# The last two heads of an attention kernel divided on chip, and seven output tiles spread between the scores

## The chip, the cores and the metric

One core of a Trainium2 chip (trn2) runs the kernel. The metric is the device time of one execution in microseconds (us), the median of several runs. TensorE multiplies matrices, VectorE, ScalarE and GpSimd work on vectors, and SyncE (SP) issues most of the DMA transfers.

## The reference

The inputs are fp32. With x of shape (2048, 512), 32 heads of 16 and a feed-forward width of 1792:

```python
q, k, v = (x @ wqkv) split into 3, by heads of 16
a = softmax(q @ k.T * 16 ** -0.5) @ v          # per head, over 2048 keys
a = concat(a) @ wo
b = (silu(x @ w1) * (x @ w3)) @ w2
g = sigmoid((x * gate_w).sum(-1))
out = g * a + (1 - g) * b
```

## The kernel before

Products with fp32 inputs are made of halves: an operand is split into a rounded part H and the rest L (type fp32r), and three matmuls (HH, HL, LH) are summed in one PSUM bank. The scores, the softmax numerators and the product with V take one or two passes.

**Order of TensorE's work.** A first stage transposes x and projects part of q and k and all of v. Then one long loop goes through a string of letters, `order`. Q is a score unit: two heads at once, 128 keys by 512 queries each, in a pair of PSUM banks `S`, followed by one exponential on ScalarE into a buffer `p` (there are 8). P multiplies two such units with V into the bank `acc`. F is a feed slot: it asks `feed` for one matmul in each of the two 64-row halves of TensorE (lanes 0 and 1). A long period is `one`: 8 Q, 21 F and 4 P, the P all at its end. A double period is `two`: 8 Q, 15 F and 4 P, the P in two groups. There are 1024 score units: 2 halves of the queries, 16 pairs of heads (`j`), 16 key blocks, 2 groups of queries.

**The feed.** `blocks()` lists what the slots are filled with, each block a sum over `length` matmuls: 136 blocks of 12 (the other q and k, and the gate and up products of the feed-forward part), 48 of 14 (`h_product`: 16 output tiles of the feed-forward product, in three parts each), and output tiles 0 to 7 of the attention's projection with wo, 12 matmuls each (tile 7 as two sums that run side by side, `o_half`). A block runs its rows 0 to 63 in one lane and then rows 64 to 127 in the other; a small VectorE write (`tick`) stands between the two. `done` then takes the bank away. There are three banks `f`; a block may take a bank only REST = 9 ticks of the loop's clock after the bank's last block ended (`pick`), and the second turn waits GAP = 6.

**Small work.** Everything else is tied to the count of scores: loads of K and Q (`load_step`), the silu's reciprocals in pieces of 64 columns (`small`), and `stages`, lists of steps of which one runs per score, the first list first. `divide(k, half)` divides the outputs of a group of 8 heads: denominators from `D_d`, one reciprocal, to `R_d`, back broadcast, a product on GpSimd, and to `N_d`. `rest_of_o` then fetches and splits groups 0 to 2 of the second half of the queries.

**Pairs.** `evac(j, half)` copies `acc` to `u` and stores 16 rows of output and one of denominators per head and query group.

**The end.** After the loop the last group of heads (k = 3, half 1) goes the way through DRAM (`reciprocals`, `fetch_o`), while TensorE does output tiles 8 to 15 with `three`: first groups 0 to 2 of all tiles (72 matmuls, into eight banks), then group 3 (24), and `mix` adds each tile to its feed-forward part and stores it.

Of the kernel before, what the change touches and what calls it, by code (L numbers as in the profile page):

```python
# [17 lines left out]
P = 128  # L18
# [15 lines left out]
def gated_mix_kernel(ctx: ExitStack, tc: tile.TileContext, x, wqkv, wo, w1, w3, w2, gate_w, out):  # L34
# [527 lines left out]
    def h_done(t, part):  # L562
        def done(ps):
            if part == 0:
                y_[t] = wk.tile([P, 512], F32, name=f"y{t % 2}")
                nc.vector.tensor_scalar(y_[t], ps, omg[:, t:t + 1], None, op0=OP.mult)
                return
            y = y_[t]
            nc.vector.scalar_tensor_tensor(y, ps, omg[:, t:t + 1], y, op0=OP.mult, op1=OP.add)  # L569
            if part == 1:  # L570
                return
            nc.sync.dma_start(B_d[P * t:P * t + P, :], y)
            if t in (11, 12, 13):
                load_bt(t - 11)
            if t in (4, 5, 6):
                later.append(lambda: load_wo((0, 1, 3)[t - 4]))
            if t == NT - 1:
                stages.append(rest_of_o())
        return done
# [20 lines left out]
    def fetch_o(k, b, o, r, e=nc.sync):  # L600
        e.dma_start(o, O_d[P * k:P * k + P, 512 * b:512 * b + 512])
        src = R_d[8 * k:8 * k + 8, 512 * b:512 * b + 512]
        nc.sync.dma_start(r, bass.AP(tensor=src.tensor, offset=src.offset, ap=[[S, 8], [0, DH], [1, 512]]))

    def divide(k, half):
# [18 lines left out]
        if (k, half) == (2, 1):  # L624
            load_wo(2)
# [14 lines left out]
    def o_half(t):  # L640
        def product(ps, r, n, second):
            k, i = divmod(n, 3)
            return nc.tensor.matmul(ps, ot[t][i == 1][r, P * k:P * k + P], wo_[k][i == 2][r, :],  # L643
                                    start=n == 0, stop=n == 3 * ND - 1)
# [6 lines left out]
    def first_half_done(t):  # L651
        def done(ps):
            nc.vector.scalar_tensor_tensor(bt[t], ps, g[:, t:t + 1], bt[t], op0=OP.mult, op1=OP.add)
# [13 lines left out]
    def load_o(k, b):  # L667

        if k not in Oh:
            Oh[k] = xp.tile([P, 2, 512], F32R, name=f"xH{k}")  # L670
            Ol[k] = xp.tile([P, 2, 512], F32R, name=f"xL{k}")
        halves_of(N_d[P * k:P * k + P, 512 * b:512 * b + 512], Oh[k][:, b - 2, :], Ol[k][:, b - 2, :], "fr")

    def rest_of_o():
        for k in range(ND - 1):
            for b in (2, 3):
                load_o(k, b)
                for _ in range(4):
                    yield

    def blocks():
# [14 lines left out]
        for t in range(NT // 2 - 1):  # L696
            yield o_product(t), o_done(t), 3 * ND
        t = NT // 2 - 1
        yield o_half(t), (first_half_done(t), o_done(t)), 3 * ND

    NBLOCK = 8 * len(chunks) + 3 * NT + NT // 2 + 1
    source = blocks()

    REST, GAP = 9, 6
# [53 lines left out]
    def evac(j, half):  # L758
        u = wk.tile([P, 512], F32, name="u")
# [7 lines left out]
        for gq in range(2):  # L767
            t = 1024 * half + 512 * gq
            for h in range(2):
                r = 32 * (2 * gq + h)  # L770
                hh = 2 * j + h
                last = half == 1 and j == NPAIR - 1
                (nc.scalar if last else nc.sync).dma_start(O_d[DH * hh:DH * hh + DH, t:t + 512], u[r:r + DH, :])
# [29 lines left out]
    LONG, SHORT = 80, 47  # L803
# [7 lines left out]
    for i, c in enumerate(order):  # L811
        clock += 1 if c != "P" else 4
        if c == "Q":
# [10 lines left out]
            if issued % 128 == (40 if issued // 128 == 5 else 12) and 1 <= issued // 128 < 8:  # L824
                stages.append(divide((issued // 128 - 1) % 4, (issued // 128 - 1) // 4))
            if small or later and hurry:
# [15 lines left out]
    assert lanes[0] is None  # L842
    for _ in reciprocals(ND - 1, 1):
        pass
    k = ND - 1
    orr = [(slot("fr", F32), slot("sg", F32)) for _ in range(2)]
    for b in (2, 3):
        fetch_o(k, b, *orr[b - 2], nc.scalar)
# [3 lines left out]


    banks = {}
    for t in range(NT // 2, NT):
        n, r = divmod(t - NT // 2, 2)
        if n < 2:
            if r == 0:
                both = psum2()
            banks[t] = both[:, r, :]  # L860
        else:
            banks[t] = bank() if t < NT - 1 else acc
        if r == 0:
            y = wk.tile([P, 2, 512], F32, name=f"p{free.pop(0)}")
        bt[t] = y[:, r, :]
        nc.sync.dma_start(bt[t], B_d[P * t:P * t + P, :])

    def project(t, k):
        o = P * t - 1024
        hi, lo = (x[k][:, 0:2, :].rearrange("p b t -> p (b t)")[:, o:o + P] for x in (Oh, Ol))  # L870
        three(banks[t], hi, lo, wo_[k][0], wo_[k][1], k == 0, k == ND - 1)

    for t in range(NT // 2, NT):
        for n in range(ND - 1):
            project(t, n)
    Oh[k], Ol[k] = (wk.tile([P, 2, 512], F32R, name=f"p{free.pop(0)}") for _ in range(2))
    for b in (2, 3):
        o, r = orr[b - 2]
        nc.vector.tensor_mul(o, o, r)
        nc.scalar.activation(Oh[k][:, b - 2, :], o, AF.Copy)  # L880
        nc.vector.tensor_sub(Ol[k][:, b - 2, :], o, Oh[k][:, b - 2, :])

    for n, t in enumerate((8, 10, 12, 13, 14, 15, 9, 11)):
        project(t, k)
        if n < NT // 2 - 1:
            mix(t, banks[t], (nc.sync, nc.scalar)[n % 2])
        else:
            mix(t, banks[t], nc.scalar, slice(0, D // 2))
            mix(t, banks[t], nc.sync, slice(D // 2, D))
# [27 lines left out]
```

## Time and profile before

| | |
|---|---|
| median of 3 runs | 1403.1 us (1402.82 to 1404.16) |
| the profiled execution | 1403.17 us, span 1401.4 us |
| busy share of the span | TensorE 100%, ScalarE 74%, VectorE 35%, GpSimd 23% |
| start of the last matmul | 1396.84 us |
| granted clock, mean | 1.000 |

The times come from runs of the whole program; the profile is one execution, whose span runs from its first to its last instruction. Matmuls overlap and their ends are modelled, so the distance between their starts says more than their busy share.

### The profile page before, as it was taken

What the parts mean: (1) busy time and instruction counts of PE and PEld (TensorE: products, weight loads), DVE (VectorE), ACT (ScalarE), POOL (GpSimd) and SP (SyncE); (2) the same over time, 40 slices, a digit from 0 to 9 for tenths busy, and PEclk for the clock granted to TensorE, in tenths of its full rate; (3) what the DMA queues carried; (4) which work ended last, traced back from release to release, by engine and by line L of the source; (5) the groups of instructions that cost most, each with busy time, mean ns of one, the idle gap of its engine ahead of it and who ended that gap; (6) DMA issues with size and microseconds to landing.
All of it is one profiled execution on the core that took longest, in us unless ns stands there. A gap on an engine that the chain in (4) does not pass through costs nothing.

```text
span 1401.4 us, 28854 instructions
## 1 busy us (share of the span) xinstructions
PE 1394.9 (100%) x11422; PEld 823.2 (59%) x11422; DVE 484.9 (35%) x1071; ACT 1032.5 (74%) x1153; POOL 320.9 (23%) x357
## 2 busy tenths in 40 slices
PE   9999999999999999999999999999999999999998
PEld 8866566566566565565565565565555555555556
DVE  5511111564545546555454654511101111101113
ACT  4457677777777777777777777787887788788771
POOL 6123433011011101110110116432242331323220
PEclk9999999999999999999999999999999999999999
DMA  7653554343224423223333246443443443445435
GB/s 207 170 122 93 139 135 113 73 113 77 47 56 84 114 55 83 63 67 96 70 77 68 80 80 165 115 97 79 106 113 79 109 102 62 111 104 133 107 95 178
DMA packets 112814, 141.44 MB, mean 101 GB/s; under 512 B 16416, under 2 KB 70944, under 8 KB 109600
## 3 DMA queue, kind: packets, MB, share of 16 engines
q1 hardware_dynamic: 111392, 137.42, 40.7%
q8 instruction: 92, 1.51, 0.5%
q10 hardware_dynamic: 1280, 2.10, 0.4%
q14 instruction: 50, 0.41, 0.1%
HBM read 90.70 MB, written 48.76 MB: 100 GB/s over the span
## 4 chain that ended last, share of the span: by engine, by line
PE 98%; DMA 1%; POOL 0%; SPq 0%; DVE 0%; issue 0%; DVEq 0%; POOLq 0%
PE acc L779 32%; PE f L432 26%; PE S L791 19%; PE f L550 11%; PE S L199 2%; PE f L636 1%; PE f L96 1%; PE f L98 1%; PE f L97 1%; DMA gw<-r_d 1%; PE f L643 0%; PE f L165 0%; PE acc L353 0%; DMA Kt<-kH_d 0%; PE S L96 0%; PE S L97 0%
## 5 line engine op out<-in xcount | busy, mean ns | idle before, releaser
L795 ACT ACTIVATE p<-S 128x1024 f32<-128x1024 f32 x1024 | 967.3, 1026 | 302.7 <-PE S L791 293.4
L779 PE MATMUL acc<-p,V 128*17 128x512 f32 x4096 | 473.5, 594 | 0.0
L791 PE MATMUL S<-Qt,Kt 50*128 50x512 f32 x2048 | 403.7, 407 | 0.7 <-DVE V L415 0.7
L791 PEld LDWEIGHTS S<-Qt,Kt 50*128 50x128 f32 x2048 | 183.4, 184 | 182.2 <-ACT p L795 80.3
L779 PEld LDWEIGHTS acc<-p,V 128*17 128x17 f32 x4096 | 102.5, 97 | 273.0 <-issue 273.0
L463 DVE RECIPROCAL sg<-sg 128x64 f32<-128x64 f32 x448 | 209.6, 517 | 51.2 <-issue 49.2
L432 PE MATMUL f<-xH,fl 64*128 64x512 f32 x1088 | 218.0, 392 | 0.1
L432 PE MATMUL f<-xL,fh 64*128 64x512 f32 x1088 | 218.0, 392 | 0.0
L432 PE MATMUL f<-xH,fh 64*128 64x512 f32 x1088 | 217.1, 390 | 0.0
L432 PEld LDWEIGHTS f<-xH,fl 64*128 64x128 f32 x1088 | 105.0, 186 | 24.3 <-POOL fl L329 0.5
L432 PEld LDWEIGHTS f<-xL,fh 64*128 64x128 f32 x1088 | 105.1, 186 | 22.3
L432 PEld LDWEIGHTS f<-xH,fh 64*128 64x128 f32 x1088 | 104.3, 185 | 23.4
L752 DVE MEMSET tick<- 1x1 f32 x191 | 11.3, 59 | 271.1 <-PE f L550 151.2
L328 POOL CAST fh<-fr 128x512 fp32r<-128x512 f32 x34 | 21.9, 645 | 356.4 <-DMA fr<-in_B_w_dram 241.4
L550 PE MATMUL f<-xH,fl 64*128 64x512 f32 x208 | 74.1, 390 | 0.0
L550 PE MATMUL f<-xL,fh 64*128 64x512 f32 x208 | 71.9, 390 | 0.0
L550 PE MATMUL f<-xH,fh 64*128 64x512 f32 x208 | 70.5, 391 | 0.0
L455 DVE COPY gs<-f 128x512 f32<-128x512 f32 x56 | 38.7, 691 | 69.8 <-PE f L432 63.5
L569 DVE SCALAR_TENSOR_TENSOR y<-f,omg,y 128x512 f32<-128x512 f32 x32 | 24.0, 752 | 107.4 <-PE f L550 107.4
L550 PE MATMUL f<-xH,raw 64*128 64x512 f32 x192 | 59.3, 390 | 0.0
L619 POOL TENSOR_TENSOR hx<-hx,gw 128x512 f32<-128x512 f32 x8 | 10.3, 1287 | 198.3 <-DMA gw<-r_d 187.9
L461 DVE TENSOR_SCALAR sg<-sg 128x512 f32<-128x512 f32 x56 | 26.2, 468 | 83.1 <-ACT sg L460 78.9
(214 smaller groups left out, 1339.7 us busy)
## 6 DMA issues: line engine op xcount, KB each, us to landing
Kt<-kH_d SPq DMA_DIRECT2D x128, 128.0 KB
h_d<-sg SPq DMA_DIRECT2D x56, 256.0 KB
sg<-h_d SPq DMA_DIRECT2D x43, 256.0 KB
fr<-in_B_w_dram SPq DMA_DIRECT2D x42, 256.0 KB
Qt<-qH_d SPq DMA_DIRECT2D x128, 64.0 KB
Kt<-kL_d SPq DMA_DIRECT2D x64, 128.0 KB
Qt<-qL_d SPq DMA_DIRECT2D x64, 64.0 KB
b_d<-y SPq DMA_DIRECT2D x16, 256.0 KB
```

The costliest lines, as they stand in the source:

```text
L96: nc.tensor.matmul(ps, sH, mH, start=first, stop=False)
L199: nc.tensor.matmul(ps[:, i, :], w[i][h][:, k, :], xs[b][:, k, :], start=n == 0, stop=n == len(order) - 1)
L328: nc.gpsimd.tensor_copy(hi, src)
L432: return nc.tensor.matmul(ps, w[i == 1][r, k, :], (xL if i == 2 else xH)[b][r, k, :], start=n == 0 and not second, stop=n == 3 * ND - 1 an ...
L455: nc.vector.tensor_copy(gs, ps)
L461: small.append(lambda: nc.vector.tensor_scalar(sg, sg, 1.0, None, op0=OP.add))
L463: small.append(lambda q=q: nc.vector.reciprocal(sg[:, q:q + 64], sg[:, q:q + 64]))
L550: ins = nc.tensor.matmul(ps, hs[t][q][i == 1][r, P * o:P * o + P], (w2L if i == 2 else w2H)[q][r, o, :], start=n == 0 and not second, stop ...
L569: nc.vector.scalar_tensor_tensor(y, ps, omg[:, t:t + 1], y, op0=OP.mult, op1=OP.add)
L779: nc.tensor.matmul(acc[r:r + DH + 1, :], V[:, k, 2 * j + h, :], p[:, h, :], start=k == 0, stop=k == NT - 1)
L791: nc.tensor.matmul(ps[:, h, :], Kt[i][r:r + 50, P * k:P * k + P], Qt[i][r:r + 50, t:t + 512], start=True, stop=True)
L795: nc.scalar.activation(p, ps, AF.Exp, scale=SCALE)
```

## The change

LONG goes from 80 to 90 and SHORT from 47 to 37. REST goes from 9 to 7. Output tile 7 becomes an ordinary block. Tiles 8 to 14 enter the feed with the first three of four groups of heads (LATE = 9 matmuls; tile 14 as two sums side by side), and their sums are added into `bt`, which `rest_of_o` loads. wo's block 2 is loaded by `later`. The last group of heads is divided in two ways: heads 24 to 29 by `six_heads` inside the loop, through DRAM; heads 30 and 31 (rows 96 to 127 of the group) after the loop, without DRAM: `acc` is copied to `u`, turned by transposes so that the queries are on partitions, divided there, turned back and split. The end does all of tile 15 and the last group of tiles 8 to 14.

```diff
-            if t in (4, 5, 6):
-                later.append(lambda: load_wo((0, 1, 3)[t - 4]))
+            if t in (4, 5, 6, 7):
+                later.append(lambda: load_wo((0, 1, 3, 2)[t - 4]))
...
-        if (k, half) == (2, 1):
-            load_wo(2)
...
-    def o_half(t):
+    def part_product(t, turns):
         def product(ps, r, n, second):
             k, i = divmod(n, 3)
-            return nc.tensor.matmul(ps, ot[t][i == 1][r, P * k:P * k + P], wo_[k][i == 2][r, :],
-                                    start=n == 0, stop=n == 3 * ND - 1)
+            return nc.tensor.matmul(ps, o_rows(t, k, i == 1)[r, :], wo_[k][i == 2][r, :],
+                                    start=n == 0 and not second, stop=n == LATE - 1 and (second or not turns))
         return product
 
...
+    sums = None
+
+    def part_done(t):
         def done(ps):
-            nc.vector.scalar_tensor_tensor(bt[t], ps, g[:, t:t + 1], bt[t], op0=OP.mult, op1=OP.add)
+            add = lambda: nc.vector.scalar_tensor_tensor(bt[t], ps, g[:, t:t + 1], bt[t], op0=OP.mult, op1=OP.add)
+            add() if sums is None else sums.append(add)
         return done
...
+    def o_rows(t, k, low):
+        x = (Ol if low else Oh)[k]
+        b, o = divmod(P * t - 1024, 512)
+        return x[:, b, o:o + P]
 
     def rest_of_o():
+        for n, x in zip("HL", (Oh, Ol)):
+            for m in range(2):
+                both = xp.tile([P, 4, 512], F32R, name=f"x{n}{m}")
+                x[2 * m], x[2 * m + 1] = both[:, 0:2, :], both[:, 2:4, :]
+        for m, n in enumerate("HL"):
+            rows = xp.tile([P, 4, 512], F32, name=f"x{n}2")
+            for i in range(4):
+                bt[NT // 2 + 4 * m + i] = rows[:, i, :]
         for k in range(ND - 1):
             for b in (2, 3):
-                load_o(k, b)
+                halves_of(N_d[P * k:P * k + P, 512 * b:512 * b + 512], Oh[k][:, b - 2, :], Ol[k][:, b - 2, :], "fr")
                 for _ in range(4):
                     yield
+        for t in range(NT // 2, NT):
+            nc.sync.dma_start(bt[t], B_d[P * t:P * t + P, :])
+            yield
+
+    def six_heads():
+
+        k, rr = ND - 1, slice(0, 6 * DH)
+        rows = lambda d: d[8 * k:8 * k + 6, 1024:2048].rearrange("h (a t) -> h a t", a=16)
+        nc.sync.dma_start(dd[rr], rows(D_d))
+        for _ in range(5):
+            yield
+        nc.vector.reciprocal(dd[rr], dd[rr])
+        yield
+        nc.sync.dma_start(rows(R_d), dd[rr])
+        both = wk.tile([P, 2, 512], F32, name="od")
+        pairs = [(both[:, 0, :], both[:, 1, :]), (slot("fr", F32), slot("sg", F32))]
+        for b in (2, 3):
+            o, r = pairs[b - 2]
+            nc.sync.dma_start(o[rr], O_d[P * k:P * k + 6 * DH, 512 * b:512 * b + 512])
+            src = R_d[8 * k:8 * k + 6, 512 * b:512 * b + 512]
+            nc.sync.dma_start(r[rr], bass.AP(tensor=src.tensor, offset=src.offset, ap=[[S, 6], [0, DH], [1, 512]]))
+        for _ in range(6):
+            yield
+        for b in (2, 3):
+            o, r = pairs[b - 2]
+            nc.gpsimd.tensor_mul(o[rr], o[rr], r[rr])
+            split(Oh[k][rr, b - 2, :], Ol[k][rr, b - 2, :], o[rr])
+            yield
 
...
-        for t in range(NT // 2 - 1):
+        for t in range(NT // 2):
             yield o_product(t), o_done(t), 3 * ND
-        t = NT // 2 - 1
-        yield o_half(t), (first_half_done(t), o_done(t)), 3 * ND
-
-    NBLOCK = 8 * len(chunks) + 3 * NT + NT // 2 + 1
+        for t in range(NT // 2, NT - 2):
+            yield part_product(t, True), part_done(t), LATE
+        yield part_product(NT - 2, False), (part_done(NT - 2), part_done(NT - 2)), LATE
+
+    LATE = 3 * (ND - 1)
+    NBLOCK = 8 * len(chunks) + 3 * NT + NT // 2 + NT // 2
     source = blocks()
 
-    REST, GAP = 9, 6
+    REST, GAP = 7, 6
...
     def evac(j, half):
+        if half == 1 and j == NPAIR - 1:
+            return
...
-    LONG, SHORT = 80, 47
+    LONG, SHORT = 90, 37
...
+            if issued == 64 * NPAIR - 22:
+                stages.append(six_heads())
...
-    assert lanes[0] is None
-    for _ in reciprocals(ND - 1, 1):
-        pass
-    k = ND - 1
-    orr = [(slot("fr", F32), slot("sg", F32)) for _ in range(2)]
-    for b in (2, 3):
-        fetch_o(k, b, *orr[b - 2], nc.scalar)
+    nrm = wk.tile([P, 4, 2, P], F32, name=f"p{free[0]}")
+    nc.gpsimd.memset(nrm, 0.0)
+    u = wk.tile([P, 512], F32, name="u")
+    nc.vector.tensor_copy(u[:, 0:256], acc[:, 0:256])
+    nc.scalar.activation(u[:, 256:512], acc[:, 256:512], AF.Copy)
+    sums = []
     while feed():
...
+    last = NT - 1
+
+    def project(t, k, terms=(0, 1, 2)):
+        for i in terms:
+            nc.tensor.matmul(banks[t], o_rows(t, k, i == 2), wo_[k][i == 1], start=k == 0 and i == 0 or k == ND - 1 and t < last and i == 0,
+                             stop=k == ND - 1 and i == 2)
+
+    k = ND - 1
+    banks[last] = bank()
+    turned = psum2()
+    back = psum2()
+    recip = const.tile([P, 2, 2, 4], F32, name="recip")
+
+    def turn(c):
+        for i in (2 * c, 2 * c + 1):
+            nc.tensor.transpose(turned[:, 0, P * i:P * i + P], u[:, P * i:P * i + P], ident)
+
+    def divided(c):
+        src = turned[:, 0, 256 * c:256 * c + 256].rearrange("p (i g r) -> p i g r", i=2, g=4)
+        nc.vector.reciprocal(recip[:, c], src[:, :, :, DH])
+        for i in range(2):
+            nc.vector.tensor_mul(nrm[:, 2 * c + i, :, P - 2 * DH:P].rearrange("p a (h d) -> p a h d", h=2),
+                                 src[:, i, :, 0:DH].rearrange("p (a h) d -> p a h d", h=2),
+                                 recip[:, c, i, :].rearrange("p (a h) -> p a h", h=2)[:, :, :, None].to_broadcast([P, 2, 2, DH]))
+
+    def turn_back(c):
+        for i in (2 * c, 2 * c + 1):
+            for a in range(2):
+                nc.tensor.transpose(back[:, a, P * i:P * i + P], nrm[:, i, a, :], ident)
+
+    def rounded(c):
+        rr, cc = slice(P - 2 * DH, P), slice(256 * c, 256 * c + 256)
+        nc.scalar.activation(Oh[k][rr, :, cc], back[rr, :, cc], AF.Copy)
+        nc.vector.tensor_sub(Ol[k][rr, :, cc], back[rr, :, cc], Oh[k][rr, :, cc])
+
+    project(last, 0, (0,))
+    turn(0)
+    turn(1)
+    divided(0)
+    divided(1)
+    for add in sums:
+        add()
+    project(last, 0, (1, 2))
+    project(last, 1, (0,))
+    turn_back(0)
+    turn_back(1)
+    rounded(0)
+    rounded(1)
+    project(last, 1, (1, 2))
+    project(last, 2)
+    banks[8], banks[9], banks[12] = turned[:, 1, :], acc, bank()
+    for two in ((8, 9), (12, 13), (10, 11), (14, 15)):
+        if two[0] == 12:
+            both = psum2()
+            banks[13], banks[10] = both[:, 0, :], both[:, 1, :]
+        elif two[0] == 10:
+            both = psum2()
+            banks[11], banks[14] = both[:, 0, :], both[:, 1, :]
+        for terms in ((0, 1), (2,)):
+            for t in two:
+                project(t, k, terms)
+        for n, t in enumerate(two):
+            if t < last:
+                mix(t, banks[t], (nc.sync, nc.scalar)[n])
+            else:
+                mix(t, banks[t], nc.scalar, slice(0, D // 2))
+                mix(t, banks[t], nc.sync, slice(D // 2, D))
```

## Rows read from the trace of the kernel before

**Rows 1.** The page: busy time of each engine, and the granted clock by slices.

```profile
PE 1394.9 (100%) x11422; PEld 823.2 (59%) x11422; DVE 484.9 (35%) x1071; ACT 1032.5 (74%) x1153; POOL 320.9 (23%) x357
...
PEclk9999999999999999999999999999999999999999
```

**Rows 2.** The chain that ended last: start us, us, engine, tile, line.

```profile
79.89 0.70 DVE V L415
80.60 0.91 PE S L791 x4
...
87.68 3.56 PE acc L779 x32
...
94.46 0.70 PE f L432 x6
...
917.05 3.56 PE acc L779 x32
...
927.81 1.84 PE acc L779 x16
...
1360.84 1.84 PE acc L779 x16
...
1373.64 1.60 PE f L643 x6
```

**Rows 3.** Timeline of the end: start us, us, engine, line, operation, out<-in, form.

```profile
1365.91 0.39 PE L636 MATMUL f<-xL,raw 64*128 64x512 f32 x1
...
1366.35 0.75 DVE L648 SCALAR_TENSOR_TENSOR bt<-f,g,bt 128x512 f32<-128x512 f32 x1 [5.88 <-PE f L636]
...
1373.71 0.69 DVE L760 COPY u<-acc 128x512 f32<-128x512 f32 x1 [4.76 <-PE acc L779]
...
1375.17 0.50 PE L96 MATMUL S<-xH,xH 128*128 128x512 f32 x1
...
1376.70 0.61 SPq L593 DMA_DIRECT2D dd<-d_d  x1
...
1387.31 0.69 DVE L879 TENSOR_TENSOR fr<-fr,sg 128x512 f32<-128x512 f32 x1 [6.36 <-DMA sg<-r_d]
...
1396.59 1.56 DVE L648 SCALAR_TENSOR_TENSOR p<-S,g,p 128x512 f32<-128x512 f32 x3
...
1396.84 0.39 PE L98 MATMUL S<-wo,p 128*128 128x512 f32 x1
```

**Rows 4.** Groups by line and form: count, busy us, mean ns, idle us before.

```profile
L463 DVE RECIPROCAL sg<-sg 128x64 f32<-128x64 f32 x448 | 209.6, 517 | 51.2 <-issue 49.2
...
L514 POOL TENSOR_TENSOR fl<-sg,fh 128x512 fp32r<-128x512 f32 x25 | 32.1, 1286 | 2.0
...
L880 ACT ACTIVATE p<-fr 128x512 fp32r<-128x512 f32 x2 | 1.3, 634 | 18.4 <-DVE fr L879 18.4
...
L143 POOL MEMSET V<- 128x512 f32 x1 | 1.0, 1000 | 0.0
L648 DVE SCALAR_TENSOR_TENSOR p<-S,g,p 128x256 f32<-128x256 f32 x2 | 0.9, 480 | 0.0
...
L407 DVE RECIPROCAL g<-g 128x16 f32<-128x16 f32 x1 | 0.3, 253 | 0.0
...
L406 DVE TENSOR_SCALAR g<-g 128x16 f32<-128x16 f32 x1 | 0.2, 176 | 0.3 <-ACT g L405 0.3
```

**Rows 5.** Timeline of TensorE in the first 12 us.

```profile
5.00 0.82 PE L165 MATMUL f<-ident,xn 128*128 128x128 f32 x3
...
10.70 0.39 PE L199 MATMUL S<-xL,wh 128*128 128x512 f32 x1
10.93 0.38 PE L165 MATMUL f<-ident,xn 128*128 128x128 f32 x2
11.15 0.38 PE L165 MATMUL S<-ident,xn 128*128 128x128 f32 x2
```

**Rows 6.** Tile f, who waited for it: us, times.

```profile
  DVE gs L455: 63.5, 47
```

More of the change, by code (lines that the diff above doesn't have):

```diff
@@ L598, in reciprocals, with fetch_o @@
         nc.sync.dma_start(rows(R_d), dd)
-    def fetch_o(k, b, o, r, e=nc.sync):
-        e.dma_start(o, O_d[P * k:P * k + P, 512 * b:512 * b + 512])
+    def fetch_o(k, b, o, r):
+        nc.sync.dma_start(o, O_d[P * k:P * k + P, 512 * b:512 * b + 512])
         src = R_d[8 * k:8 * k + 8, 512 * b:512 * b + 512]
@@ L649, in mix @@
         e.dma_start(out[P * t:P * t + P, c], bt[t][:, c])
-    def first_half_done(t):
+    sums = None
+    def part_done(t):
         def done(ps):
-            nc.vector.scalar_tensor_tensor(bt[t], ps, g[:, t:t + 1], bt[t], op0=OP.mult, op1=OP.add)
+            add = lambda: nc.vector.scalar_tensor_tensor(bt[t], ps, g[:, t:t + 1], bt[t], op0=OP.mult, op1=OP.add)
+            add() if sums is None else sums.append(add)
         return done
@@ L665, in gated_mix_kernel @@
     Oh, Ol = {}, {}
[L667 to L672, printed above, removed]
-    def rest_of_o():
+    def o_rows(t, k, low):
+        x = (Ol if low else Oh)[k]
+        b, o = divmod(P * t - 1024, 512)
+        return x[:, b, o:o + P]
+    def rest_of_o():
+        for n, x in zip("HL", (Oh, Ol)):
[6 more added lines that the diff above has]
+                bt[NT // 2 + 4 * m + i] = rows[:, i, :]
         for k in range(ND - 1):
             for b in (2, 3):
-                load_o(k, b)
+                halves_of(N_d[P * k:P * k + P, 512 * b:512 * b + 512], Oh[k][:, b - 2, :], Ol[k][:, b - 2, :], "fr")
                 for _ in range(4):
                     yield
+        for t in range(NT // 2, NT):
[24 more added lines that the diff above has]
+            yield
     def blocks():
@@ L771, in evac @@
                 hh = 2 * j + h
-                last = half == 1 and j == NPAIR - 1
-                (nc.scalar if last else nc.sync).dma_start(O_d[DH * hh:DH * hh + DH, t:t + 512], u[r:r + DH, :])
+                nc.sync.dma_start(O_d[DH * hh:DH * hh + DH, t:t + 512], u[r:r + DH, :])
     def pv(two):
@@ L854, in gated_mix_kernel @@
     banks = {}
[L855 to L889, printed above, removed]
+    last = NT - 1
```

## The prediction

> **What bounds the kernel now.** I read the shares by engine first, then the chain of waits, then the timeline of the last 40 us. TensorE is busy 1394.9 of 1401.4 us [rows 1], and ScalarE, next, 74%; so the question is whether TensorE ever waits. A busy matmul isn't a matmul at full pace, so I looked at distances. In the chain every burst of the second attention product (acc, L779) stands the same distance after the one before. In the long periods (21 feed slots, 8 scores, 8 units of P times V) 79 distances between the bursts at 87.68 and 917.05 give 10.498 us each; in the double periods (15 feed slots, the same 8 scores and units) 46 distances between 927.81 and 1360.84 give 9.414 us [rows 2]. Nothing but the order of TensorE's own work sets these. A feed slot, which is two matmuls of 64 rows side by side, takes 0.23 us: three of them 0.70 [rows 2].
>
> After the last burst come six lone feeds in 1.60 us [rows 2], then the 96 closing matmuls, the first at 1375.17, the last at 1396.84: 95 steps of 0.228 us [rows 3], with no gap. The division of the last heads, from the load of the denominators at 1376.70 to the first multiplication at 1387.31, takes 10.6 us of round trips through DRAM [rows 3] and is hidden behind them. So the tail too is bound by TensorE, and the kernel's end lies 4.6 us after the start of the last matmul: last additions on VectorE, stores, end of program.
>
> The profiled execution took 1403.17 us, 1.77 more than its span; the median of the runs shown is 1403.1. I add to 1403.17 and take 0.1 off at the end.
>
> **The change, part by part.**
>
> *Slots and work.* Before: 80×21+7+47×15+15 = 2407 slots; the work is 136 blocks of 12, 48 of 14 and 8 output tiles of 12, together 2400. After: 90×21+7+37×15+15 = 2467 slots; the work is 2400 + 6 tiles×9 + 9 for tile 14, which runs its two row halves in two banks side by side, = 2463. It fits. Going through the rules of `pick` slot by slot, the lone feeds left behind the last burst are six before (as the chain shows) and two after.
>
> *Ten double periods become long ones.* Each costs 10.498 − 9.414 = 1.084 us, in all **+10.8 us**. A long period buys six more slots for that, 0.18 us each and not 0.23: it has one burst of P times V and not two. Both lengths are means over nearly the whole of their phase, so this term has little width.
>
> *63 of the 96 closing matmuls leave the tail:* 63×0.228 = −14.4 us. Four lone feeds fewer at 0.23: −0.9. Together **−15.3 us**.
>
> *What enters the tail, on TensorE or in front of it.* Time 0 is the end of the last burst.
> - Twelve transposes of 128 columns. At the kernel's start pairs of them stand 0.22 us apart, 0.11 each, and the first comes 0.23 after the matmul before it, like any matmul [rows 5]: +1.3.
> - The copy of acc, halved between VectorE and ScalarE. The whole copy started 0.1 after the burst (1373.71 against 1373.64) and took 0.69 [rows 2, 3]; 256 columns took VectorE 0.27 less than 512 in the closing addition (0.48 against 0.75) [rows 3, 4], so a half takes some 0.42 and is there at about 0.55. Two lone feeds and one closing matmul keep TensorE until about 0.8. +0.1, from 0 to 0.3.
> - The division. Per half one reciprocal of 8 and two products of 64 values a row; nearest rows: reciprocal of 16 values 0.25, a small operation on 16 values 0.18 [rows 4], to which 48 more values add 0.05 at the rate of the line above. So 0.25+2×0.23 = 0.7 a half. The first half can start at about 1.5, is done at 2.2, the second at 2.9. TensorE has three matmuls of cover, to about 2.1, then waits 0.1 to 0.2, turns four back until 2.75 and waits again. +0.4, from 0 (operations at 0.15) to 1.5 (at 0.4 each).
> - The split of the last 32 rows: ScalarE 0.63 [rows 4], VectorE 0.69, with the addition of tile 14's second half, 0.75, queued ahead of it. First half ready at about 4.4; the five covering matmuls end at about 4.6. 0, up to 0.7 if the division is late.
> - A new wait: tiles 13 and 10 go into the pair of banks that holds tile 8. Tile 8's last product is the fifth matmul of the end, tile 13's first the ninth, 0.91 later; an addition is done 1.19 after the start of its last matmul (1365.91 to 1367.10) [rows 3]. All later matmuls queue behind it. +0.3, from 0 to 0.4.
> - Tiles now end in pairs, so tile 15's two half additions stand behind tile 14's whole one: +0.4, from 0 to 0.7. The stores are as many and as big.
>
> Together **+2.5 us**, bounds 1.3 and 4.9.
>
> *Moved at no cost, and by what cover.* The division of the first six heads of the last group starts at score 1002 and is used from score 1014 on, 12 scores or 14 us later (a score per 9.414/8 us); the same round trip took 10.6 us [rows 3]. Behind it GpSimd has two products and two splits, 6.4 us by 1.29 an operation and about half that for the cast [rows 4], then the clearing of `nrm`, twice the 1.00 us of the 512-column clearing [rows 4]; that one can only start when the last burst gives its buffer free, 2.6 us before time 0, so it ends at −0.6, 2 us before it is needed. On SP's queue the six loads of O and eight of B (those 8 leave the tail) stand between scores 949 and 981, the fetches of this division behind the stores of pair 14; the first product that needs them comes at score 989. In the ten new long periods a tile of the feed-forward product (42 slots) lasts 21.0 us and not 26.4; that is the lead with which its pieces of h are fetched again, against 2 us for a piece's split [rows 4] and its landing. wo's third block only moves from one idle place to another. If one of these covers fails, TensorE waits for the difference.
>
> *REST from 9 to 7.* A bank may be written again 7 slots after its last product, 1.63 us, not 9. Going through the rules, 16 blocks then meet exactly 7 and 32 meet 8. An evacuation ends 1.19 us after its last matmul starts where VectorE is free [rows 3], which it was in 47 of 56 copies of L455, since these waited for TensorE [rows 6]; the release itself costs little (VectorE's copy ended at 80.59, the matmul stands at 80.60 [rows 2]). 0.4 us to spare: no cost.
>
> **Sum:** 10.8 − 15.3 + 2.5 = −2.0 us, bounds −3.2 and +0.4: 1403.17 − 2.0 − 0.1 = **1401.1 us**, own range 1399.9 to 1403.5. That is 0.14%, and 0.2% (2.8 us) is about what a measurement of this kernel tells from no change. The gain of 15 us in the tail is real, but ten longer periods pay most of it back, because TensorE was full in both places.
>
> **The rivals.**
> 1. *All waits of the tail hide.* Nothing is added but the transposes: −3.2 us, 1399.9. For it: the fillers are placed at each wait. Against: three matmuls of cover are 0.7 us and six small VectorE operations 1.4. It passes 0.2% once 0.8 of the 1.2 us of waits that I count are hidden. Chance 0.20.
> 2. *Slower: banks come free too late.* Place: every block that takes a bank after 7 or 8 slots, all through the feed-forward phase, where reciprocals of 0.52 us [rows 4] stand in VectorE's queue. It decides from the point where evacuation and release together exceed 1.63 us, 0.44 more than where VectorE is free. With one reciprocal (0.52) ahead 16 blocks lose 0.08 each, 1.3 us; with two ahead it is 16×0.60 + 32×0.37, 21 us. Half of the blocks behind one and a tenth behind two: +2.8, 1403.9. With a fifth behind two it is +4.9, 1406.0, the point from which the kernel is measurably slower. Against: 47 of 56. Chance of over 0.2% slower 0.10.
> 3. *Slower: the prepared six heads are late.* GpSimd does its 6.4 us and the 2 us clearing in order; from score 1002 to time 0 there are about 30 us, and the clearing is wanted at 1.5. So it decides from a fetch of 23 us in place of 10.6; one of 28 would cost the 5 us that make the kernel measurably slower, 1406, since TensorE has no more fillers. Against: no loads of Q and K are left on SP's queue by then. Chance 0.03.
> 4. *Slower: the clock.* The kernel's first transposes stand 0.21 us apart, later ones 0.11 [rows 5]: at the program's start TensorE runs at half pace (1.2 and not 2.4 GHz), though the row of granted clocks reads full there too [rows 1]. If the waits of the tail bring that back, the last 24 matmuls take 0.23 more each: +5 or so, 1406. Against: nothing like it later in the trace, and my waits are below 1 us together. Chance 0.04. The Trainium skill (TensorE: Matmul & The Clock Gate, section on what's actually happening) has the throttled clock as the default, which activity releases; the trace agrees in the pace of the first transposes.
>
> **How the numbers follow.** Forecast and its neighbourhood within 0.2%: 0.63. Rival 1: 0.20. Rivals 2 to 4: 0.17. So faster 0.20, same 0.63, slower 0.17. No way leads far below 1399.9, so the range begins at 1399.6; upwards it goes to 1405.0, which holds the sum's upper bound and the milder half of rival 2.
>
> **What would show it.** The bursts of acc still 10.50 and 9.41 us apart, with the last about 10.8 us later than now; TensorE's last matmul start 10 us, not 23, after the end of the last burst; waits of TensorE on VectorE in the tail of tenths, one at tile 13's first matmul. Periods longer than 10.50, with waits for evacuations, would prove rival 2; a wait for GpSimd behind `nrm` rival 3; closing steps of 0.4 us rival 4. If the distance from the last burst to the end is below 14 us, I have set the tail's waits too high.

## The result, and the profile of the changed kernel

The changed kernel takes **1409.28 us** (median of 6 runs, 1407.56 to 1409.64) against 1403.55 us for the kernel before, measured beside it (6 runs, 1402.82 to 1405.22). The ratio is 1.0036, with an interval of 1.0023 to 1.0049. It is slower by more than the 0.2% that can be told from no change, and 4.3 us above the upper end of the forecast range. The profiled execution is the shortest of the six: 1407.56 us, with a span of 1405.7; the spans of the others are 1405.9 to 1407.4.

The page of the kernel after: the shares by engine, and the granted clock by slices:

```profile
PE 1394.4 (99%) x11497; PEld 825.5 (59%) x11497; DVE 488.8 (35%) x1089; ACT 1033.9 (74%) x1154; POOL 329.0 (23%) x364
...
PEclk9999999999999999999999999999999999999999
```

TensorE is as busy as in [rows 1], though the span is 4.3 us longer: the time went into gaps, not into work. The granted clock is full up to 1404.0 us, which is after the last matmul (the mean over the span is 0.999). The list of waits names the larger gaps. First TensorE's list in the kernel after (line, what it waited for, us in total, times, the longest):

```profile
PE S L897 <- DVE xL L646: 1.6, 1, 1.6
PE acc L353 <- DVE acc L349: 1.6, 1, 1.6
PE f L550 <- DVE tick L789: 1.3, 1, 1.3
PE S L897 <- DVE xH L646: 1.3, 1, 1.3
PE S L829 <- DVE V L415: 0.7, 1, 0.7
```

The same list of the kernel before has only the second and the last of these:

```profile
PE acc L353 <- DVE acc L349: 1.6, 1, 1.6
PE S L791 <- DVE V L415: 0.7, 1, 0.7
```

Three waits are new: two in the closing matmuls (L897), and one in the loop, behind a tick (the one-element write on VectorE that lets the second half of a block start, L789). The list counts only time in which no matmul of TensorE runs; where one of the two lanes waits and the other works, it is silent.

**The loop.** The chain of the kernel after, at its first burst, in the middle and at its end (start us, us, what):

```profile
87.40 3.56 PE acc L817 x32
...
799.83 1.11 PE f L432 x6
...
959.66 3.56 PE acc L817 x32
...
972.44 3.70 DMA Kt<-kH_d
976.16 4.91 DMA dd<-d_d
981.09 0.55 DVE dd L596
...
981.72 0.49 PE f L550
982.45 3.56 PE acc L817 x32
...
992.95 3.56 PE acc L817 x32
...
1374.26 1.84 PE acc L817 x16
...
1383.70 3.56 PE acc L817 x32
```

Most long periods take 10.48 to 10.51 us (982.45 to 992.95 here) and the double ones 9.42 on the mean (9.44 here), nearly as in [rows 2]. But between 959.66 and 982.45 there are two long periods in 22.79 us, 1.8 more than 21.0. In that stretch the chain leaves TensorE and runs through a load of denominators and its reciprocal on VectorE. VectorE's timeline there:

```profile
981.09 0.55 DVE L596 RECIPROCAL dd<-dd 128x64 f32<-128x64 f32 x1 [4.50 <-DMA dd<-d_d]
981.59 0.26 DVE L789 MEMSET tick<- 1x1 f32 x2
```

The reciprocal is issued five scores after its load. The load went out on SP's queue at 976.16, behind loads of Q and K, and took 4.91 us to land. For 4.50 us VectorE had nothing to do but wait in order, and two ticks stood behind the reciprocal. One of them was what TensorE's next block half needed. The kernel before has the same wait, on the same instruction, and a longer one:

```profile
976.32 0.55 DVE L596 RECIPROCAL dd<-dd 128x64 f32<-128x64 f32 x1 [5.22 <-DMA dd<-d_d]
976.82 0.06 DVE L752 MEMSET tick<- 1x1 f32 x1
```

There it fell into double periods, and the bursts around it (965.51, 974.92, 984.34 in its chain) stand 9.41 and 9.42 us apart: nothing was lost.

```profile
974.92 1.84 PE acc L779 x16
...
984.34 1.84 PE acc L779 x16
```

A smaller loss stands at 799.83 in the chain of the kernel after: six feed matmuls take 1.11 us there in place of 0.70, and their period 10.94. One lane's first product waits until the copy that empties its bank is over, at 800.33:

```profile
799.65 0.68 DVE L455 COPY gs<-f 128x512 f32<-128x512 f32 x1
```

All eight traces with REST 7 have this period, at 10.92 to 10.94 us; the two of the changed kernel with REST 9 (experiments 3 and 7) don't.

**The tail.** Timeline of the kernel after from the last burst on (start us, us, engine, line, operation, form; in brackets the idle time before it and what ended that), TensorE's rows first:

```profile
1387.19 0.50 PE L641 MATMUL f<-wo,xL 64*128 64x512 f32 x1
...
1391.57 0.63 PE L897 MATMUL S<-wo,xH 128*128 128x512 f32 x2
...
1393.50 0.71 PE L897 MATMUL S<-wo,xH 128*128 128x512 f32 x2
...
1396.26 1.17 PE L897 MATMUL S<-wo,xH 128*128 128x512 f32 x4 [1.59 <-DVE xL L646]
...
1399.16 0.72 PE L897 MATMUL S<-wo,xH 128*128 128x512 f32 x2 [1.28 <-DVE xH L646]
...
1400.41 0.40 PE L897 MATMUL f<-wo,xL 128*128 128x512 f32 x1
```

and VectorE's:

```profile
1387.33 0.42 DVE L885 COPY u<-acc 128x256 f32<-128x256 f32 x1 [4.00 <-PE acc L817]
1388.82 0.21 DVE L912 RECIPROCAL recip<-S 128x8 f32<-128x8 f32 x1 [1.07 <-PE S L908]
1389.14 0.35 DVE L914 TENSOR_TENSOR p<-S,recip 128x64 f32<-128x64 f32 x2
...
1392.65 0.70 DVE L926 TENSOR_TENSOR xL<-S,xH 32x512 fp32r<-32x512 f32 x1 [0.66 <-ACT xH L925]
1393.38 0.75 DVE L646 SCALAR_TENSOR_TENSOR xH<-S,g,xH 128x512 f32<-128x512 f32 x1
...
1395.37 0.74 DVE L646 SCALAR_TENSOR_TENSOR xL<-S,g,xL 128x512 f32<-128x512 f32 x1
1397.69 1.41 DVE L646 SCALAR_TENSOR_TENSOR xH<-S,g,xH 128x512 f32<-128x512 f32 x2 [1.58 <-PE S L897]
1400.62 0.75 DVE L646 SCALAR_TENSOR_TENSOR xL<-S,g,xL 128x512 f32<-128x512 f32 x1 [1.51 <-PE S L897]
```

Tile 10's first product (1396.26) starts when the addition of tile 13 (1395.37 to 1396.11) is over; tile 14's (1399.16) when the addition of tile 11 has ended, the second of the two that begin at 1397.69 and end at 1399.10. Tiles 13 and 10 are the two banks of one pair that the kernel takes as one buffer, and so are 11 and 14. In each pair the second mate is written for the first time after the first mate has been handed to VectorE. Tile 13's own first product (1393.50) comes about 0.2 us late. It starts behind the second subtraction, which reads the two banks of `back` and ends at 1393.36, and not behind tile 8's addition, which runs from 1393.38 to 1394.13.

**Where the 4.3 us of the two spans come from.** Both executions are cut at the start of the first matmul of the first burst, of the last burst, and of the first matmul after it (T0 below).

| stretch, us | before | after | difference | forecast |
|---|---|---|---|---|
| start to first burst | 87.6 | 87.3 | −0.3 | 0 |
| first to last burst | 1282.4 | 1296.3 | +13.9 | +10.8 |
| last burst | 3.56 | 3.56 | 0 | 0 |
| T0 to the end | 27.8 | 18.5 | −9.3 | −12.8 |
| span | 1401.4 | 1405.7 | +4.3 | −2.0 |

The forecast is missed by 3.1 us in the loop and 3.5 us in the tail, less 0.3 at the start. The medians differ by 5.7 us, 1.4 more than the spans, because the profiled execution was the changed kernel's shortest. One source of such spread is the start, at which none of the edits is aimed: up to the first burst the twelve traces of this case take 87.3 to 88.8 us, whatever the version. So the stretches of a trace say more about an edit than its whole span.

### The profile page after: what moved, and what is told of

Same layout as the page of the kernel before. It is cut to its first block, busy times and chain, and to the rows that moved or that the text cites. A ratio compares the mean times of both kernels' runs of the same rounds, so it can differ in the third digit from the quotient of the medians.

```text
span 1405.7 us, 29024 instructions
## 1 busy us (share of the span) xinstructions
PE 1394.4 (99%) x11497; PEld 825.5 (59%) x11497; DVE 488.8 (35%) x1089; ACT 1033.9 (74%) x1154; POOL 329.0 (23%) x364
## 4 chain that ended last, share of the span: by engine, by line
PE 98%; DMA 1%; DVE 1%; SPq 0%; issue 0%; ACT 0%; DVEq 0%; ACTq 0%
PE acc L817 32%; PE f L432 27%; PE S L829 19%; PE f L550 11%; PE f L634 2%; PE S L199 2%; PE f L641 1%; PE f L96 1%; PE f L98 1%; PE f L97 1%; DMA dd<-d_d 0%; PE acc L353 0%; PE f L165 0%; DMA Kt<-kH_d 0%; PE S L165 0%; DVE xL L646 0%
## 5 line engine op out<-in xcount | busy, mean ns | idle before, releaser
L432 PE MATMUL f<-xH,fl 64*128 64x512 f32 x1088 | 220.6, 395 | 0.0
L432 PE MATMUL f<-xL,fh 64*128 64x512 f32 x1088 | 219.6, 393 | 0.0
L432 PE MATMUL f<-xH,fh 64*128 64x512 f32 x1088 | 217.9, 389 | 0.0
L789 DVE MEMSET tick<- 1x1 f32 x198 | 11.7, 59 | 283.4 <-PE f L550 144.4
L550 PE MATMUL f<-xH,fh 64*128 64x512 f32 x208 | 57.5, 392 | 0.0
L550 PE MATMUL f<-xL,fh 64*128 64x512 f32 x208 | 56.2, 392 | 0.0
L550 PE MATMUL f<-xH,fl 64*128 64x512 f32 x208 | 55.4, 392 | 0.0
L513 POOL CAST fh<-sg 128x512 fp32r<-128x512 f32 (+1 forms) x32 | 18.1, 567 | 147.1 <-DMA sg<-h_d 83.3
```

The source lines that it names most:

```text
L432: return nc.tensor.matmul(ps, w[i == 1][r, k, :], (xL if i == 2 else xH)[b][r, k, :], start=n == 0 and not second, stop=n == 3 * ND - 1 an ...
L513: nc.gpsimd.tensor_copy(hi, r[:, 0:n])
L550: ins = nc.tensor.matmul(ps, hs[t][q][i == 1][r, P * o:P * o + P], (w2L if i == 2 else w2H)[q][r, o, :], start=n == 0 and not second, stop ...
```

## The experiments

Theory A has two causes: (1) the pairing of banks costs the tail about 3 us, (2) the late reciprocal holds the ticks and costs the loop about 2 us or more. Theory B says that the waits of the tail are covered by VectorE's additions and the stores, which are late anyway, so that removing them returns nothing. Theory C puts the loop's excess on the shorter rest of the banks (REST 7). Each ratio is against the kernel before on the same chip, whose median was 1403.98 for the first four, 1403.86 for the next four and 1403.90 for the last two. The changed kernel stood beside 1403.55, so a difference to it is good to about 0.4 us at best.

**1. Other banks in the tail, so that both mates of a pair are written before either is read.**

```diff
-    banks[8], banks[9], banks[12] = turned[:, 1, :], acc, bank()
+    banks[8], banks[9], banks[12], banks[13] = turned[:, 1, :], acc, bank(), bank()
...
-        if two[0] == 12:
+        if two[0] == 10:
             both = psum2()
-            banks[13], banks[10] = both[:, 0, :], both[:, 1, :]
-        elif two[0] == 10:
-            both = psum2()
-            banks[11], banks[14] = both[:, 0, :], both[:, 1, :]
+            banks[10], banks[11] = both[:, 0, :], both[:, 1, :]
+        elif two[0] == 14:
+            banks[14] = psum2()[:, 0, :]
```

> Tiles 13, 10, 11 and 14 get other banks (13 a bank f of its own, 10 and 11 the first pair together, 14 half of the second pair), nothing else changes. Theory A, shared banks: at the end TensorE waited twice, 1.6 and 1.3 us by the list of waits, because a tile's first product counted the addition of the tile in the other half of its pair; both waits and the short one at tile 13 go, the last matmul starts about 10 us after the last burst in place of 13.2, and the time falls by about 3.2 us, to some 1406. Theory B, the end is held by VectorE's additions or by the stores and the banks only show it: the waits move elsewhere, and less than 1 us is won. Theory C, the short rest, speaks only of the loop: no difference.

Measured: 1406.49 us, ratio 1.0016 (1.0007 to 1.0025), 2.8 us below the changed kernel. The two waits of L897 are gone from the list and T0 to the end took 15.5 us instead of 18.5. Nine of the eleven times lie below the changed kernel's shortest. The profiled execution is the longest of the eleven, and its loop lost more than that of the changed kernel: two late periods of 12.63 and 12.20 us, 3.8 over their due. Only the first, 2.1 over, is the wait for the tick (1.65 us on TensorE). In the second the granted clock reads 0.5, which is 1.2 GHz, for 3.41 us, and the burst there takes 5.26 us in place of 3.56. That is 1.7 us more. The rows are the burst in the chain and that stretch (us, busy time of each engine, granted clock, DMA):

```profile
983.39 5.26 PE acc L817 x32
...
984.21:987.62 3.41, 3.41 (x23) 0.78 (x19) 0.00 (x0) 0.30 (x1) 1.47 (x2) 0.50 0.49 151
```

In the changed kernel's profiled execution, where TensorE stood for 1.29 us at the same place, the granted clock stays at 1.00.

**2. The reciprocals five scores later**, so that VectorE reaches them when their data has landed.

```diff
         nc.sync.dma_start(dd, rows(D_d))
-        for _ in range(5):
+        for _ in range(10):
             yield
         nc.vector.reciprocal(dd, dd)
```

> In the division by way of DRAM, ten scores in place of five lie between the load of the denominators and the reciprocal; all else as in the changed kernel. Theory A: the one period of 12.27 us (a reciprocal that waited 4.5 us for its load held VectorE's queue, and with it the tick that lets a block's second half start) goes back to 10.5, about 1.8 us less, some 1407.5. Theory C, the short rest stretches periods: the 12.27 stays or another appears, no difference in time.

Measured: 1406.67 us, ratio 1.0019 (1.0010 to 1.0028), 2.6 us below the changed kernel; all eleven times lie below that kernel's shortest. The loop took 1294.5 us instead of 1296.3, and the tail 18.5 with both waits, as it should. VectorE's timeline of this kernel shows the ticks in front of the reciprocal, which waits 0.83 us and holds none of them up:

```profile
981.07 0.06 DVE L789 MEMSET tick<- 1x1 f32 x1 [1.58 <-PE f L550]
981.96 0.55 DVE L596 RECIPROCAL dd<-dd 128x64 f32<-128x64 f32 x1 [0.83 <-DMA dd<-d_d]
```

**3. REST 9 again in the changed kernel.**

```diff
-    REST, GAP = 7, 6
+    REST, GAP = 9, 6
```

> REST back from 7 to 9, all else as in the changed kernel. Theory C, banks released too late cost the loop its surplus of about 3 us over the forecast: the loop gets shorter by 1 to 3 us. Theory A: REST costs the loop nothing, four more lone feeds stand behind the last burst (six, not two), which is +0.9 us, and the late reciprocal may fall differently since the blocks stand differently (0 to -1.8).

Measured: 1408.09 us, ratio 1.0028 (1.0018 to 1.0039), 1.2 below the changed kernel, with intervals that overlap. Its long periods keep the same length (10.504 us on the mean in both, those with a stall left out). Its loop of 1295.1 has one late period of 11.46 us, 1.0 over, again behind a tick, but at another place and for another reason. It begins at 813.5, in the feed-forward phase, where the tick stands behind a product of the silu that takes 1.83 us (0.72 in the changed kernel) and a copy:

```profile
821.19 1.83 DVE L481 TENSOR_TENSOR sg<-raw,sg 128x512 f32<-128x512 f32 x1
...
823.57 0.06 DVE L789 MEMSET tick<- 1x1 f32 x1
```

Why that product was slow here is open. The reciprocal of the denominators waits 4.59 us for its load here too, and costs TensorE nothing: the longer rest moved the blocks against it. Of the 1.2 us between this loop and the changed kernel's 1296.3, 0.4 is the bank's wait of REST 7; the rest is the late reciprocal's 1.8 less this 1.0. The other periods didn't get shorter.

**4. Edits 1 and 2 together.**

> Other banks for tiles 13, 10, 11 and 14 and ten scores ahead of the reciprocal, together. Theory A: the two savings add, -5.0 us against the changed kernel, some 1404.3, which is the kernel before to within 1 us; the forecast of 1401.1 then still misses 2 to 3 us, which lie in the loop's slow drift and in what lies outside the span. Theory B or C: less than 2.5 us in all.

Measured: 1403.24 us, ratio 0.9998 (0.9989 to 1.0008), 6.0 us below the changed kernel; 2.8 and 2.6 make 5.4, so the two savings add within the spread. TensorE's list of waits has nothing left of the loop or of the tail (the one lane's wait of REST 7, which the list can't show, is still there, in a period of 10.92):

```profile
PE acc L353 <- DVE acc L349: 1.5, 1, 1.5
PE S L829 <- DVE V L415: 0.8, 1, 0.8
PE f L165 <- DMA xn<-in_A_x_dram: 0.2, 1, 0.2
```

Its loop took 1294.7 us. In its tail the products run through, and the additions have no gaps; TensorE's rows stand in the first block, VectorE's last ones in the second:

```profile
1385.84 0.50 PE L641 MATMUL f<-wo,xL 64*128 64x512 f32 x1
...
1392.96 1.07 PE L897 MATMUL S<-wo,xH 128*128 128x512 f32 x4
...
1395.45 0.39 PE L897 MATMUL f<-wo,xL 128*128 128x512 f32 x1
```

```profile
1394.67 1.40 DVE L646 SCALAR_TENSOR_TENSOR xH<-S,g,xH 128x512 f32<-128x512 f32 x2
1395.99 0.74 DVE L646 SCALAR_TENSOR_TENSOR xL<-S,g,xL 128x512 f32<-128x512 f32 x1
1396.65 0.87 DVE L646 SCALAR_TENSOR_TENSOR xL<-f,g,xL 128x256 f32<-128x256 f32 x2
```

The last matmul starts 9.6 us after T0 (13.2 in the changed kernel), and the end comes 15.5 after it.

**5. Of edit 1 one pair put back**: tile 10 as the mate of 13, and tile 11 in the bank that 13 had; all else as in 4.

```diff
-    banks[8], banks[9], banks[12], banks[13] = turned[:, 1, :], acc, bank(), bank()
+    banks[8], banks[9], banks[12], banks[11] = turned[:, 1, :], acc, bank(), bank()
...
-        if two[0] == 10:
+        if two[0] == 12:
             both = psum2()
-            banks[10], banks[11] = both[:, 0, :], both[:, 1, :]
+            banks[13], banks[10] = both[:, 0, :], both[:, 1, :]
```

> The combined version (other banks, reciprocal ten scores later) with one of the shared pairs put back: tile 10 again in the other half of tile 13's pair; tiles 11 and 14 stay apart. Theory A, a first product waits for the addition of its bank mate: the wait of 1.6 us ahead of tile 10 and the 0.3 ahead of tile 13 come back and nothing else, the last matmul starts 1.6 to 2.0 us later, 1404.9 or so. Theory B, additions and stores hold the end and hide such a wait: less than 0.7 us.

Measured: 1405.36 us, ratio 1.0011 (1.0002 to 1.0020), 2.1 above experiment 4, and the tail is 17.1, 1.7 above. The wait comes back at the one place, with the same length, on TensorE's timeline:

```profile
1395.87 0.70 PE L897 MATMUL S<-wo,xH 128*128 128x512 f32 x2 [1.60 <-DVE xL L646]
```

This is the pairing by itself. Theory B is refuted: 1.6 us of this wait and 1.7 us of the tail go together.

**6. The tiles of the end one at a time**, with all else as in 4, so that the last additions spread.

```diff
-        for terms in ((0, 1), (2,)):
-            for t in two:
-                project(t, k, terms)
+        for t in two:
+            project(t, k)
```

> The combined version, but the last 24 matmuls go tile by tile (three terms of a tile in a row), not two tiles at a time. If the pairing costs what the prediction gave it (0.4 us, since tile 14's addition stands ahead of tile 15's halves), the time falls by 0.4. If the row of eight additions on VectorE, which stand back to back behind the second rounding, holds the end, the order of the products changes nothing.

Measured: 1404.14 us, ratio 1.0002 (0.9993 to 1.0011), no gain. VectorE's last two operations are over 11.7 us after T0 either way: it works through its additions without a gap from 6.2 us after T0 on, in the one order as in the other. What follows them differs without an edit to it: the end comes 4.4 us after VectorE's last operation here, and 3.8 in experiment 4.

**7. Experiment 4 with REST 9** (edit of 3).

> The combined version with REST 9 in place of 7. Theory A and the prediction: the periods keep their lengths and four more lone feeds stand in the tail, +0.9 us. Theory C, short rest costs the loop: the loop is shorter and the time not longer.

Measured: 1404.5 us, ratio 1.0005 (0.9996 to 1.0014), 1.3 us above experiment 4, with overlapping intervals. In the traces 1.2 of the 1.3 is the start up to the first burst (88.8 us against 87.6), which varies as much with REST 7. The loop is 1294.1, 0.6 shorter, of which 0.4 is the bank's wait that is gone; the tail is 16.1, 0.6 longer, since four more feeds stand in it. So the two values cost the same. Theory C, an excess of 1 to 3 us from the short rest, falls; what is left of it is 0.4 us in one period.

**8. Edit 2 in the kernel before**, as a control.

> The kernel before with only the ten scores in place of five ahead of the reciprocal. Control: if the late reciprocal is a loss that came with the change (the load was issued in a long period now, in a double one before), the kernel before gains nothing, at most the 0.35 us of its one period of 10.85. If it was a loss of both kernels, this one falls by 1.5 us or more and the combined version's comparison with before is flattered.

Measured: 1403.48 us, ratio 1.0000 (0.9991 to 1.0010). The late reciprocals cost the kernel before nothing that can be measured: one period of 10.85 us in its chain becomes 10.50, and in that one TensorE waited behind GpSimd, not behind a tick. So what edit 2 returns in the changed kernel is a loss that came with the change.

**9. Two of the closing additions taken off VectorE**, all else as in 4: ScalarE multiplies tiles 9 and 13 by the gate, GpSimd adds, and SP stores them.

```diff
-            if t < last:
+            if t in (9, 13):
+                y = wk.tile([P, 2, 512], F32, name=f"p{free[1 + t // 13]}")[:, 0, :]
+                nc.scalar.activation(y, banks[t], AF.Copy, scale=g[:, t:t + 1])
+                nc.gpsimd.tensor_add(y, y, bt[t])
+                nc.sync.dma_start(out[P * t:P * t + P, :], y)
+            elif t < last:
```

> The combined version, with two of the eight last additions (tiles 9 and 13) taken from VectorE: ScalarE multiplies by the gate, GpSimd adds. If VectorE's row of additions holds the end (it ran without a gap from the second rounding on), the last addition ends 0.7 to 1.3 us earlier, 1402.3 or so in the terms of the combined version's 1403.2; TensorE's last matmul is then the bound. If the stores hold the end, the additions end earlier and the time stays.

Measured: 1404.54 us, ratio 1.0003 (0.9994 to 1.0012), no gain. VectorE's last rows of this kernel:

```profile
1395.52 1.41 DVE L646 SCALAR_TENSOR_TENSOR xH<-S,g,xH 128x512 f32<-128x512 f32 x2 [0.84 <-PE S L897]
...
1397.51 0.86 DVE L646 SCALAR_TENSOR_TENSOR xL<-f,g,xL 128x256 f32<-128x256 f32 x2
```

VectorE now waits 0.84 us for tile 10's products, and its last operations start 10.7 us after T0 (1386.85) in place of 10.8: two additions fewer moved the last one by 0.1. What is then last is the products themselves, and behind them one addition each for tiles 10, 11 and 14 and the two halves of 15. The tail is 16.1 us all the same, 0.7 longer than in experiment 4, since 4.6 us follow VectorE's last operation, and not 3.8. So VectorE alone doesn't hold the end; what lengthens the last stretch is open.

**10. Experiment 9 with both of ScalarE's roundings ahead of VectorE's subtractions.**

```diff
     rounded(0)
     rounded(1)
+    rest(0)
+    rest(1)
```

Here `rounded` keeps the activation alone and `rest` holds the subtraction.

> The same, and the two halves of the last split are written so that both ScalarE roundings stand ahead of both VectorE subtractions. ScalarE's second rounding waited 0.76 us for VectorE's first subtraction, though they touch different columns. If that wait is on the path, 0.3 to 0.7 us less again; if the subtraction then waits for both roundings in turn, nothing changes.

Measured: 1404.81 us, ratio 1.0006 (0.9997 to 1.0015). ScalarE's pair runs without the 0.76 us wait between its two, VectorE's pair starts only when both are done (1390.48), and the subtractions end at 1391.8, 5.9 after T0, in place of 6.2. The end doesn't move.

No version beats the kernel before. Experiment 4 equals it.

## Why the prediction was wrong

**The step that failed first: "A new wait".** The prediction saw that a bank which is taken again brings a wait, named one of them, tile 13's behind tile 8's addition, and gave it 0.3 us, at most 0.4. That wait isn't there: tile 13's first product starts at 1393.50, while tile 8's addition still runs until 1394.13. What is there, 0.2 us behind the second subtraction, fits tiles 13 and 10 standing in the pair `back`. The two waits that cost were not in the sum. A pair is one buffer, so tile 10's first product waits for whoever reads the pair then, which is the addition of its mate 13, and in the other pair 14 waits for 11's. The two read 1.59 and 1.28 us on the timeline, and with some 0.5 us to get going again they delay the last matmul by 3.4 us more than in experiment 4 (13.2 against 9.6, less tile 13's 0.2). At the end of the kernel 3.1 remain, as VectorE catches up in the gaps. Experiment 1 takes both waits away, experiment 5 brings one back.

**The second: "Moved at no cost".** The list of what ten more long periods move holds the loads, the six heads, the pieces of h and wo's third block, but not the reciprocals of an earlier division. The reciprocal waits for its load in VectorE's queue in both kernels, 5.22 and 4.50 us; where it falls against the block halves decides whether TensorE needs a tick behind it. The price was 1.8 us in the profiled execution, 2.1 in that of experiment 1, where 1.7 us at the lower clock followed, and nothing in that of experiment 3. The row was there to read in the trace of before. Why the price differs between executions, and whether this or the start explains that the changed kernel's other times lie up to 2.1 us above the profiled one, stays open, since no trace shows those executions.

**The third: "REST from 9 to 7 ... no cost", and "ten double periods" at 1.084.** The shorter rest costs 0.4 us, in the one period where a bank was still being emptied. Apart from this and the late reciprocal the loop is longer than forecast by about 0.9 us (1294.1 in experiment 7, against 1282.4 before, is 11.7 and not 10.8). The long periods have a mean of 10.504 us against 10.494 in the kernel before, each without its stalled ones, and the double ones 9.42 against 9.41. It is there with REST 9 too. I didn't find what lengthens them. Nor is every distance before set by TensorE's own order alone, as the prediction has it: one of the 79 is the 10.85 of experiment 8.

**What held.**
- The 63 matmuls and four lone feeds that leave the tail: two lone feeds (products of the feed that run after the loop) stand behind the last burst, as counted, and the rest of the products run 0.23 us apart, as those of [rows 3].
- The front of the tail. With the banks apart the last matmul starts 9.6 us after T0; the forecast was 10, of which 0.3 was the wait for tile 8, which these banks don't have. The reciprocal of 8 values took 0.21 us, two products 0.35; the first product of the last rows stands 4.4 us after T0 (1391.57), where the sum had 4.6 for the end of its cover.
- The tail as a whole, but for the two waits: mended it is 15.5 us against 15.0 forecast. Its last term was under-priced, and its reason isn't borne out: from the last matmul's start to the end it is 5.8 us in experiment 4 and 4.5 before, 1.3 more and not 0.4. Tiles that end in pairs aren't the reason, since experiment 6 parts them and gains nothing. Of the 1.3, 0.8 is VectorE's row of additions, which ends 2.1 us after that start, 1.3 before; the rest comes behind VectorE's last operation (3.8 us, 3.2 before).
- Rival 1 (all waits hide) is out by the list of waits; rival 2, at the size it would need, by experiments 3 and 7: what it describes happens once, for 0.4 us; rival 3 by GpSimd, which was idle for 7.29 us before it cleared `nrm` at 1384.81, 2.4 us ahead of T0; rival 4 by the full clock and steps of 0.23 in the tail (the lower clock came once, in the loop of experiment 1).

The slower outcome came, in the main, by none of the ways to which its chance was given. The forecast was right that the tail's 15 us are mostly paid back by the ten periods, and experiment 4 shows it: with both mistakes of the change mended, and a tail that is 12.4 us shorter, the time is that of the kernel before.

## What to carry to other kernels

List for every buffer that is taken again who reads it last, and take a pair of banks as what it is for the program, one buffer: write both mates before either is read. When work around an in-order queue shifts, look in the trace of before for instructions that wait there long at no cost today, and ask what stands behind them. A stall can also cost more than its own length: in experiment 1 the lower clock followed it. And where the engine that bounds the kernel is full in both places, moving work pays only the difference of its prices, here 0.23 us a matmul in the tail against 0.18 a slot in the loop, less every wait that the new place brings.

## What was not expected of the hardware

The copy of acc was halved between VectorE and ScalarE to run side by side, but ScalarE's half began at 1387.79, when VectorE's, from 1387.33, was over (0.42 us). The same holds for the two roundings: ScalarE's second half waited 0.76 us for VectorE's subtraction on other columns of the same banks. The Trainium skill (PSUM — Partial Sum Buffer, section on bank collisions) says that two engines must not be in one bank and the same partitions at once, whatever their columns; the trace agrees in so far as the program makes them take turns; no run here lets them go at once. By that rule the two mates of a pair are different banks and could go side by side; that they don't (1.59 and 1.28 us) lies in the pair being one buffer for the program, since there is no wait where both mates are written before either is read (experiments 1 and 4).
